# Agent attention and two MoE layers on one core: a query softmax with tokens on partitions, weight conversion in halves without GpSimd, filler products in the prologue

## The chip, the core and the metric

The kernel runs on one core of one Trainium2 chip. The metric is the device time of one execution in microseconds. Engines are named as in the profile: PE (TensorE) multiplies, PEld is its weight load, DVE (VectorE) and ACT (ScalarE) do elementwise work, POOL (GpSimd) does some of it too, and SP (SyncE) issues the DMAs.

## The reference

What is computed, cut to its core (12480 tokens, 128 channels, 49 agents, hidden width 2048):

```
def sm(a, b):                                  # softmax of scaled scores
    s = (a @ b.transpose(0, 2, 1)) / sqrt(128)
    s = s - s.max(-1, keepdims=True)
    e = exp(s)
    return e / (e.sum(-1, keepdims=True) + 1e-9)
agent_v = sm(agents, k) @ v                    # 49 x 128
x = sm(q, agents) @ agent_v                    # 12480 x 128
h = maximum(x @ w_in1, 0);  x = (h * h) @ w_out1
h = x @ w_in2;  g = maximum(h, 0) + alpha * minimum(h, 0);  out = g @ w_out2
```

The four weight matrices come as 64-bit floats; all else, and the output, is 32-bit.

## The kernel before, in words

The first stage computes the agent attention over k and v, 13 chunks of tokens (one of 192, twelve of 1024), with a running maximum. Its result, `avT`, is folded into the first weight matrix (`w1_product`: `agent_v @ w_in1`), so that the main loop starts from the softmax weights of the queries. The second layer's linear part (`alpha * h`) is folded into a small matrix M, the product of `w_in2` scaled by alpha with `w_out2` (`m_transpose`, `m_alpha`, `m_product`, `m_add`); `w_out2` itself is scaled by one minus alpha.

The main loop runs over 25 blocks of queries (320 tokens, 23 times 512, 384), each with 8 steps `s`. A step does four products on PE, in this order: `H1` (hidden of layer 1, 2 x 128 hidden units), `O1` (layer 1's output, two steps behind), `H2` (layer 2's hidden, eleven steps behind) and `O2` (layer 2's output, one behind `H2`). Every factor is split into a high and a low part in a 32-bit format for PE (`F32R`), and each product is the sum of three (low x high, high x low, high x high); a contraction uses 64 rows of the array, so two products run side by side (`mm2`, pairs of matmuls). Between them ACT does `R1` (relu), `SQ` (square) and `G2_hi`, and DVE does `G1_hi`, `G1_lo` and `G2_lo` (the splits).

The softmax weights of block b+1 are made during block b. The query tile has channels and agents folded onto 32-row groups: `q_transpose` (32x32 transposes on DVE), `q_split_hi`, `q_split_lo`, `q_scores` (six pairs of matmuls, 256 columns each), `q_squares` (two DVE transposes out of PSUM), `q_max` with `swap` (four small copies to exchange the halves of the agents), `q_sub`, `q_exp`, `q_sum` with `swap`, `q_norm`, `q_back` (transpose), `q_hi`, `q_lo`. The tables `before` and `after` at the end of the kernel say at which step of a block each stands.

Everything ahead of block 2 is written out by hand in the string `ORDER` (the prologue): one word for each step, run from left to right, and every engine gets its instructions in that order. There `K`, `V` load chunks, `T C S X P A E F M R` are the attention's steps on a chunk or group, `N0 N1 N2 vT vc W Y Z` its end and the folded weights, and a word such as `bwi2.1` is a step on a piece of a weight: `d` load, `a` and `b` the conversion of the 64-bit words to 32-bit floats (`w_abs` on ACT, three integer instructions of `w_bits` on DVE), `s` scale (POOL), `h` and `l` the high and low part (ACT; POOL, two of them on DVE), `v` swap of halves by DMA, `t y z w` the matrix M. A weight has four pieces of 512 columns. `H1_16` is the first step after `ORDER`.

PSUM has a two-bank tile for each of the tags `h1`, `h2`, `o1`, `o2`; the query scores use `h1`, so the next `H1` waits until they are read. POOL and DVE both work on the weights in SBUF during the prologue.

Of the kernel before, what the change touches and what calls it, by code (L numbers as in the profile page):

```python
# [19 lines left out]
def agent_attention_moe_kernel(  # L20
# [34 lines left out]
    GA = (NA + 1) // 2  # L55
# [71 lines left out]
    raw = Slots(stg, 6, [QW, 2], I32, "raw")  # L127
    mag = Slots(stg, 2, [QW], I32, "mag")
    wf = Slots(stg, 7, [QW], F32, "wf")

    def w_load(x):
        name, g = x.split(".")
        g = int(g)
        w, t_ = W_IN[name].bitcast(I32), raw.take(x)
        if name[:2] == "wi":
            nc.sync.dma_start(
                out=t_.rearrange("p n w -> p (n w)"), in_=w[:, g * QW * 2:(g + 1) * QW * 2],
            )
        else:
            nc.sync.dma_start(  # L140
                out=t_.rearrange("p (k c) w -> p k (c w)", c=C),
                in_=w.rearrange("(k p) c -> p k c", p=128)[:, 4 * g:4 * g + 4, :],
            )

    def w_abs(x):
        nc.scalar.activation(mag.take(x).bitcast(F32), raw.get(x)[:, :, 1].bitcast(F32), AF.Abs, scale=REBIAS)

    def w_bits(x, dst):
        lo, hi, a = raw.get(x)[:, :, 0], raw.get(x)[:, :, 1], mag.get(x)
        nc.vector.tensor_scalar(a, a, 3, None, op0=ALU.logical_shift_left)  # L150
        nc.vector.scalar_tensor_tensor(  # L151
            out=a, in0=hi, scalar=SIGN, in1=a, op0=ALU.bitwise_and, op1=ALU.bitwise_or
        )
        nc.vector.scalar_tensor_tensor(
            out=dst.bitcast(I32), in0=lo, scalar=29, in1=a, op0=ALU.logical_shift_right, op1=ALU.bitwise_or
        )
        raw.drop(x)
        mag.drop(x)

    with tc.manual_schedule(), ExitStack() as first:  # L160
# [3 lines left out]
        banks["early"] = early  # L164

# [60 lines left out]
        def q_load(b, queue=None):  # L226
            if b >= NB:
                return
            q_sb[b] = qp.tile([128, NT], F32, tag="q", name="q_sb", bufs=2)[:, :QB * NQS[b]]
            n = NQS[b] // 2  # L230
            for r in range(2):
                for i in range(2):
                    p = r * H + i * QB
                    for h in range(2):
                        (queue or nc.sync).dma_start(
                            out=q_sb[b][p:p + QB].rearrange("t (h j c) -> t h j c", h=2, c=QB)[:, h],
                            in_=qv[i][:, h, Q0[b] + r * n:Q0[b] + (r + 1) * n],
                        )

        def q_transpose(b):  # L240
            if b >= NB:
                return
            t_ = qp.tile([128, NT], F32, tag="qT", name="qT", bufs=2)[:, :QB * NQS[b]]
            nc.vector.transpose(t_, q_sb[b])
            q_sb[b] = t_

        def q_split_hi(b):
            if b >= NB:
                return
            qh_sb[b] = qp.tile([128, NT], F32R, tag="qh", name="qh", bufs=1)[:, :QB * NQS[b]]  # L250
            nc.scalar.copy(qh_sb[b], q_sb[b])

        def q_split_lo(b):
            if b >= NB:
                return
            ql_sb[b] = qp.tile([128, NT], F32R, tag="ql", name="ql", bufs=1)[:, :QB * NQS[b]]
            nc.vector.tensor_tensor(out=ql_sb[b], in0=q_sb.pop(b), in1=f32(qh_sb[b]), op=ALU.subtract)

        def q_scores(b):
            if b >= NB:  # L260
                return

            n = QB * NQS[b] // 2
            p_ = ps("h1", "s2_ps")[:, :, :n]
            qh, ql = qh_sb.pop(b), ql_sb.pop(b)
            mm2(
                lambda r: p_[:, r],
                [
                    lambda r, a=a, x=x, h=h: (a[rows(r), h], x[rows(r), h * n:(h + 1) * n])
                    for h in range(2) for a, x in ((agTl, qh), (agTh, ql), (agTh, qh))  # L270
                ],
            )
            s2_ps[b] = p_

        def swap(t_):

            for i in range(4):
                o = i ^ 1
                nc.vector.tensor_copy(t_[i * QB:(i + 1) * QB, 1, :], t_[o * QB:(o + 1) * QB, 0, :])

        def q_squares(b):
            if b >= NB:
                return

            s = qp.tile([128, NT // QB, QB], F32, tag="s2", name="s2", bufs=1)[:, :NQS[b]]
            p_ = s2_ps.pop(b)
# [100 lines left out]
        def w_hi(x):  # L387
            nc.scalar.copy(halves(x)[0], source(x))
# [588 lines left out]
```

## Time and profile before

| what | value |
|---|---|
| time, median of 3 runs | 1099.97 us (1099.87 to 1102.6) |
| profiled execution, its own time | 1100.91 us |
| span of the profiled execution | 1099.1 us |
| PE busy | 1069.3 us, 97% |
| DVE busy | 892.7 us, 81% |
| ACT busy | 732.4 us, 67% |
| POOL busy | 20.6 us, 2% |
| mean granted clock of PE | 0.99 |

How to read it: the span is the time from the first to the last instruction, and the execution's own time lies 1.81 us above it. Busy shares are averages over stages with different limits. The prologue takes about the first 126 us, the loop the rest. A matmul's duration in the trace includes its passage through the array, so that matmuls overlap; what one costs in a dense stretch is the distance from its start to the next one's start. A matmul of full 32-bit floats appears in the trace as two rows (a transpose as one), and a row with "x2" stands for two matmuls that run side by side.

### The profile page before, as it was taken

To read this page: it belongs to the slowest core of one execution; us is meant where nothing else is said; L and a number is where in the kernel's file an instruction comes from. 1 tells how busy PE (TensorE), PEld (TensorE's weight loads), DVE (VectorE), ACT (ScalarE), POOL (GpSimd) and SP (SyncE) were. 2 spreads that over 40 slices of the span, in tenths; PEclk is the share of its full clock that TensorE was granted. 3 is DMA by queue.
4 is the path that set the end of the run, shared out by engine and by line. 5 is a ranking of instruction groups with operands and counts; after the bars stand their busy time and mean duration, and the time that the engine had idled before them with its cause. 6 is when DMAs were issued, how large, how long until landed. Compare 5 with 4: busy or idle time off the path is not lost.

```text
span 1099.1 us, 22054 instructions
## 1 busy us (share of the span) xinstructions
PE 1069.3 (97%) x9352; PEld 855.5 (78%) x9352; DVE 892.7 (81%) x1375; ACT 732.4 (67%) x851; POOL 20.6 (2%) x20
## 2 busy tenths in 40 slices
PE   8968999999999999999999999999999999999997
PEld 5646878888888888888888888888888888888886
DVE  7988988788788888888888788788888878878743
ACT  5857766666666676666666766666666766766642
POOL 0033000000000000000000000000000000000000
PEclk9969999999999999999999999999999999999999
DMA  9942011111111111111111111111111111001111
GB/s 331 393 105 44 17 22 36 22 25 34 29 20 31 30 19 32 29 20 30 30 21 30 30 21 29 30 20 30 30 21 30 29 18 30 20 11 30 23 23 17
DMA packets 120314, 49.24 MB, mean 45 GB/s; under 512 B 103511, under 2 KB 110232, under 8 KB 120216
## 3 DMA queue, kind: packets, MB, share of 16 engines
q1 hardware_dynamic: 120216, 47.84, 18.0%
q8 instruction: 73, 1.20, 0.5%
q14 instruction: 25, 0.20, 0.1%
HBM read 27.59 MB, written 6.39 MB: 31 GB/s over the span
## 4 chain that ended last, share of the span: by engine, by line
PE 89%; DVE 5%; DMA 2%; issue 1%; ACT 1%; SPq 1%; DVEq 0%; ACTq 0%
PE o L78 50%; PE h_ps L78 36%; PE s_ps L78 2%; DVE g1l L771 2%; DMA raw<-in_moe_w_in_dram 1%; DVE g1h L766 1%; DMA ring<-in_k_dram 1%; PE av_ps L78 1%; PE kT_ps L525 1%; DVE g2l L847 0%; PE M_ps L78 0%; DMA q_sb<-in_q_dram 0%; DVE mag L151 0%; PE e_ps L568 0%; ACT kT L531 0%
## 5 line engine op out<-in xcount | busy, mean ns | idle before, releaser
L755 ACT ACTIVATE g<-h_ps 128x1024 f32<-128x1024 f32 (+2 forms) x200 | 201.1, 1006 | 164.6 <-PE h_ps L78 162.0
L841 ACT ACTIVATE g2h<-h_ps 128x1024 fp32r<-128x1024 f32 (+2 forms) x200 | 201.5, 1008 | 154.5 <-PE h_ps L78 134.3
L847 DVE SCALAR_TENSOR_TENSOR g2l<-h_ps,g2h 128x1024 fp32r<-128x1024 f32 (+2 forms) x200 | 238.2, 1191 | 23.0 <-ACT g2h L841 23.0
L771 DVE TENSOR_TENSOR g1l<-g,g1h 128x1024 fp32r<-128x1024 f32 (+2 forms) x200 | 243.0, 1215 | 6.8
L766 DVE CAST g1h<-g 128x1024 fp32r<-128x1024 f32 (+2 forms) x200 | 137.2, 686 | 104.6 <-ACT g L759 103.8
L759 ACT ACTIVATE g<-g 128x1024 f32<-128x1024 f32 (+2 forms) x200 | 207.8, 1039 | 6.2
L78 PE MATMUL o<-g1l,wo1h 64*128 64x512 f32 (+2 forms) x800 | 157.1, 389 | 4.9 <-DVE g1l L771 4.8
L78 PE MATMUL o<-g2l,wo2h 64*128 64x512 f32 (+2 forms) x800 | 157.8, 389 | 1.7 <-DVE g2l L847 1.7
L78 PE MATMUL o<-g1h,wo1l 64*128 64x512 f32 (+2 forms) x800 | 157.8, 391 | 0.5 <-DVE g1h L766 0.3
L78 PE MATMUL o<-g2h,wo2h 64*128 64x512 f32 (+2 forms) x800 | 158.1, 389 | 0.0
L78 PE MATMUL h_ps<-xh,wi2n 64*128 64x512 f32 (+2 forms) x800 | 157.4, 389 | 0.7 <-DVE g2l L847 0.7
L78 PE MATMUL h_ps<-sh,wi2s 64*128 64x512 f32 (+2 forms) x800 | 157.6, 388 | 0.4 <-DMA sh<-xh 0.4
L78 PE MATMUL o<-g2h,wo2l 64*128 64x512 f32 (+2 forms) x800 | 157.3, 388 | 0.0
L78 PE MATMUL o<-g1h,wo1h 64*128 64x512 f32 (+2 forms) x800 | 156.7, 388 | 0.0
L78 PEld LDWEIGHTS o<-g1l,wo1h 64*128 64x128 f32 x800 | 75.8, 186 | 23.7 <-DVE g1l L771 6.8
L78 PEld LDWEIGHTS o<-g2l,wo2h 64*128 64x128 f32 x800 | 76.2, 185 | 18.7 <-DVE g2l L847 2.1
L78 PEld LDWEIGHTS h_ps<-sh,wi2s 64*128 64x128 f32 x800 | 76.7, 185 | 17.9 <-DMA sh<-xh 0.9
L78 PEld LDWEIGHTS h_ps<-xh,wi2n 64*128 64x128 f32 x800 | 76.5, 185 | 18.1 <-DVE g2l L847 1.5
L78 PEld LDWEIGHTS o<-g2h,wo2l 64*128 64x128 f32 x800 | 76.6, 186 | 17.5 <-ACT g2h L841 0.4
L78 PEld LDWEIGHTS o<-g1h,wo1l 64*128 64x128 f32 x800 | 75.6, 186 | 18.5 <-DVE g1h L766 1.3
L78 PEld LDWEIGHTS o<-g2h,wo2h 64*128 64x128 f32 x800 | 76.3, 185 | 16.7
L78 PEld LDWEIGHTS o<-g1h,wo1h 64*128 64x128 f32 x800 | 75.8, 186 | 17.2
(139 smaller groups left out, 1290.4 us busy)
## 6 DMA issues: line engine op xcount, KB each, us to landing
ring<-in_k_dram SPq DMA_DIRECT2D x12, 512.0 KB, 9.2
ring<-in_v_dram SPq DMA_DIRECT2D x12, 512.0 KB, 10.2
sh<-xh SPq DMA_DIRECT2D x46, 128.0 KB, 2.4
sl<-xl SPq DMA_DIRECT2D x46, 128.0 KB, 2.3
out_dram<-ot SPq DMA_DIRECT2D x92, 64.0 KB, 2.0
q_sb<-in_q_dram SPq DMA_DIRECT2D x176, 32.0 KB, 1.9
raw<-in_moe_w_in_dram SPq DMA_DIRECT2D x8, 512.0 KB, 9.1
raw<-in_moe_w_out_dram SPq DMA_DIRECT2D x8, 512.0 KB, 10.3
```

The source lines that it names most:

```text
L78: nc.tensor.matmul(o, lhsT, rhs, start=start, stop=stop)
L525: nc.tensor.transpose(kT_ps[c][:, j // t, (j % t) * p:(j % t + 1) * p], t_[:p, j, :], ident[:p, :p])
L755: nc.scalar.activation(g, h1p.pop(s), AF.Relu)
L759: nc.scalar.activation(h1g[s], h1g[s], AF.Square)
L766: nc.vector.tensor_copy(gh, g)
L771: nc.vector.tensor_tensor(out=gl, in0=g, in1=f32(gh), op=ALU.subtract)
L841: nc.scalar.activation(gh, h2p[s], AF.Relu)
L847: nc.vector.scalar_tensor_tensor(out=gl, in0=p_, scalar=0.0, in1=f32(gh), op0=ALU.max, op1=ALU.subtract)
```

## The change

It has five parts.

1. The query softmax has tokens on partitions. `q_scores` is now, for each 128 tokens, one matmul of full 32-bit floats with the query tile as the stationary operand and 49 agents as columns. Maximum, subtraction, sum and division then run on 49 numbers along the free axis; the two splits of the query and all `swap` copies are gone. The weights are transposed back in 32x32 squares, split, and brought to the place that the loop expects by 16 DMAs for each block (`q_place`). Block 0 and 1 are transposed on PE instead.
2. Weights are converted in halves (1024 columns), not quarters. The sign, the magnitude and the scale come from one parametric ReLU on ACT (`w_rebias`, slope -2^32 for negative numbers), so that DVE needs two integer instructions for a half (`w_shift`, `w_low_bits`) and not three for a quarter.
3. No weight work is on POOL: scaling and the low parts are on DVE, as is the scaling by alpha; three of the high parts are on DVE, three on ACT.
4. Products of a zero tile (`keep_busy`, words `@n` in `ORDER`: n matmuls of 256 columns in a 16-bit format) are put into the prologue, 86 of them.
5. The 192-token chunk of k and v comes last, not first; four of the `G1_hi` of the prologue move to ACT (`HI_SCALAR`); and `ORDER` is written anew.

The diff, cut to what matters:

```diff
+    SMALL = 12
     def chunks(x):
...
+        whole.insert(SMALL, x[0][o:o + FIRST].rearrange("(p t) c -> p (t c)", t=TS))
...
+    NWARM = 18
+    UW, UC = DFF // 2, FC // 2
+    raw = Slots(stg, 3, [UW, 2], I32, "raw")
+    wf = Slots(stg, 4, [UW], F32, "wf")
+    mts = Slots(stg, 1, [UW], F32, "mT")
...
-    def w_abs(x):
-        nc.scalar.activation(mag.take(x).bitcast(F32), raw.get(x)[:, :, 1].bitcast(F32), AF.Abs, scale=REBIAS)
-    def w_bits(x, dst):
-        lo, hi, a = raw.get(x)[:, :, 0], raw.get(x)[:, :, 1], mag.get(x)
-        nc.vector.tensor_scalar(a, a, 3, None, op0=ALU.logical_shift_left)
-        nc.vector.scalar_tensor_tensor(
-            out=a, in0=hi, scalar=SIGN, in1=a, op0=ALU.bitwise_and, op1=ALU.bitwise_or
-        )
-        nc.vector.scalar_tensor_tensor(
-            out=dst.bitcast(I32), in0=lo, scalar=29, in1=a, op0=ALU.logical_shift_right, op1=ALU.bitwise_or
-        )
+        def w_rebias(x):
+            if x[:3] != "wi1":
+                wf.take(x)
+            nc.scalar.activation(
+                single(x), raw.get(x)[:, :, 1].bitcast(F32), AF.Prelu, scale=REBIAS, alpha=-(2.0 ** 32)
+            )
+        def w_shift(x):
+            a = single(x).bitcast(I32)
+            nc.vector.tensor_scalar(a, a, 3, None, op0=ALU.logical_shift_left)
+        def w_low_bits(x):
+            a = single(x).bitcast(I32)
+            nc.vector.scalar_tensor_tensor(
+                out=a, in0=raw.get(x)[:, :, 0], scalar=29, in1=a, op0=ALU.logical_shift_right, op1=ALU.bitwise_or
+            )
+            raw.drop(x)
...
         def q_scores(b):
             if b >= NB:
                 return
-            n = QB * NQS[b] // 2
-            p_ = ps("h1", "s2_ps")[:, :, :n]
-            qh, ql = qh_sb.pop(b), ql_sb.pop(b)
-            mm2(
-                lambda r: p_[:, r],
-                [
-                    lambda r, a=a, x=x, h=h: (a[rows(r), h], x[rows(r), h * n:(h + 1) * n])
-                    for h in range(2) for a, x in ((agTl, qh), (agTh, ql), (agTh, qh))
-                ],
-            )
-            s2_ps[b] = p_
+            n = count(b)
+            s2_ps[b] = ps("h1", "s2_ps")[:, 0, :n * H].rearrange("p (j a) -> p j a", a=H)[:, :, :NA]
+            t_ = q_sb.pop(b)
+            for j in range(n):
+                mm(s2_ps[b][:, j], t_[:, j * 128:(j + 1) * 128], agT[:, :NA])
+            e_sb[b] = e_pad[b % 2][:, :n]
...
+        def q_sum(b):
+            if b >= NB:
+                return
+            sm = small_q(b, "sm")
+            nc.vector.tensor_reduce(out=sm[:, :, 0], in_=q_weights(b), op=ALU.add, axis=AX.X)
+            nc.vector.tensor_scalar(sm, sm, 1e-9, None, op0=ALU.add)
+            nc.vector.reciprocal(sm, sm)
+            mx_sb[b] = sm
...
+        def q_place(b):
...
+            for u in range(4):
+                for g in range(2):
+                    for r in range(2):
+                        p = r * H + g * QB
+                        nc.sync.dma_start(
+                            out=f32(qs_sb[b][p:p + QB, :, u * n:(u + 1) * n]),
+                            in_=f32(t_[u * QB:(u + 1) * QB, :, g * n:(g + 1) * n]),
                         )
...
         def w_scale(x):
-            g = int(x[4:])
-            nc.gpsimd.tensor_tensor(
+            nc.vector.tensor_tensor(
...
+        HI_VECTOR = "wi2.0 wo1.0 wo1.1".split()
+        LO_POOL = "".split()
...
         def m_alpha(x):
+            g = unit(x)[1]
+            nc.vector.tensor_tensor(out=by_chunk(mts.take(g)), in0=wT.pop(x), in1=of_chunk(alp, g), op=ALU.mult)
...
+        def keep_busy(n):
+            if "loop" in banks:
+                p_ = banks["fill"][:, 1]
...
+            for _ in range(n):
+                mm(p_[:, :256], warm[:, :128], warm)
...
-            bwi2.3 vT vc hwi2.3 PART1 W0 awo2.1 bwo2.0 W1 Y0 Z0 swo2.0 awo2.3 bwo2.1 PART2 H1_0 Y1 q2 r1_0
+            fwi2.1 @15 vT vc hwi2.1 bwo2.0 PART1 @6 W0 fwo2.0 awo2.1 W1 Y0 bwo2.1 Y1 Z0 Z1 PART2 @10 H1_0 q2
...
         before = {
-            0: [(q_split_lo, 1)], 2: [(q_max, 1)], 3: [(q_sub, 1)], 4: [(q_sum, 1)], 5: [(q_norm, 1)],
-            6: [(q_back, 1)], 7: [(q_lo, 1), (q_transpose, 2)],
+            2: [(q_sum, 1)], 3: [(q_norm, 1), (q_back, 1)], 4: [(q_lo, 1), (q_place, 1)], 7: [(q_transpose, 2)],
         }
-        after = {3: [(q_exp, 1)], 6: [(q_hi, 1)], 7: [(q_split_hi, 2)]}
+        after = {1: [(q_exp, 1)], 3: [(q_hi, 1)]}
...
+        HI_SCALAR = [int(x) for x in "3 5 7 9".split()]
...
             if i == 1:
                 q_scores(b + 1)
-                q_squares(b + 1)
+                q_max(b + 1)
+                q_sub(b + 1)
```

What this does to the order of instructions is shown at three places. First PE, in the loop, at the second step of a block, where the scores of the next block stand between `O1` (tile `o`, weights `wo1h`) and `H2` (tile `h_ps`, weights `wi2n`). Before:

```order
L78 MATMUL o_2254<-g1h,wo1h 128x512 x2
L78 MATMUL s_ps<-qh,agTl 128x256 x2
L78 MATMUL s_ps<-ql,agTh 128x256 x2
L78 MATMUL s_ps<-qh,agTh 128x256 x2
L78 MATMUL s_ps<-qh,agTl 128x256 x2
L78 MATMUL s_ps<-ql,agTh 128x256 x2
L78 MATMUL s_ps<-qh,agTh 128x256 x2
L78 MATMUL h_ps<-xh,wi2n 128x512 x2
```

And now:

```order
L84 MATMUL o_1624<-g1l,wo1h 128x512 x2
L84 MATMUL o_1624<-g1h,wo1h 128x512 x2
L84 MATMUL s_ps<-agT,qT 128x49 x4
L84 MATMUL h_ps<-xh,wi2n 128x512 x2
L84 MATMUL h_ps<-xl,wi2n 128x512 x2
```

Twelve matmuls of 256 columns in six pairs have become four of 49 columns, each with stationary data of its own on all 128 rows.

Second DVE, in the prologue, from the last attention result (`avT`) to the first loop steps (`g1h`, `g1l`). `W1l` is the low part of the folded weight on which `H1_0` waits. Before:

```order
L633 COPY avT<-avT_ps 128x128
L150 TENSOR_SCALAR mag<-mag 128x512
L151 SCALAR_TENSOR_TENSOR mag<-raw,mag 128x512
L154 SCALAR_TENSOR_TENSOR wf<-raw,mag 128x512
L650 TENSOR_TENSOR W1l<-w_ps,W1h 128x512
L150 TENSOR_SCALAR mag<-mag 128x512
L151 SCALAR_TENSOR_TENSOR mag<-raw,mag 128x512
L154 SCALAR_TENSOR_TENSOR wf<-raw,mag 128x512
L650 TENSOR_TENSOR W1l<-w_ps,W1h 128x512
L395 TENSOR_TENSOR wo1l<-wf,wo1h 128x512
L766 CAST g1h<-g_849 128x2x320
L771 TENSOR_TENSOR g1l<-g_849,g1h 128x2x320
```

And now:

```order
L611 COPY avT<-avT_ps 128x128
L356 TENSOR_SCALAR wf<-wf 128x1024
L360 SCALAR_TENSOR_TENSOR wf<-raw,wf 128x1024
L356 TENSOR_SCALAR wf<-wf 128x1024
L627 TENSOR_TENSOR W1l<-fill_ps,W1h 128x512
L627 TENSOR_TENSOR W1l<-w_ps,W1h 128x512
L360 SCALAR_TENSOR_TENSOR wf<-raw,wf 128x1024
L413 TENSOR_TENSOR mT<-wT_ps,alp 128x1024
L782 CAST g1h<-g_792 128x2x320
L787 TENSOR_TENSOR g1l<-g_792,g1h 128x2x320
L782 CAST g1h<-g_813 128x2x320
L787 TENSOR_TENSOR g1l<-g_813,g1h 128x2x320
```

The pieces are twice as long, one of the three conversion instructions is gone, and the scaling of the transposed weight (`mT`) has come over from ACT.

Third SP's queue in the loop, one block: `q_sb` is the load of a query block, `sh` and `sl` the swapped halves of the second layer's input, `out_dram` the result, `qs` the placed softmax weights. Before:

```order
L235 DMA q_sb<-in_q_dram 32x8x32 x8
L807 DMA sh<-xh 64x512 x2
L807 DMA sl<-xl 64x512 x2
L865 DMA out_dram<-ot 32x16x32 x4
L235 DMA q_sb<-in_q_dram 32x8x32 x8
```

And now:

```order
L223 DMA q_sb<-in_q_dram 32x16x32 x4
L823 DMA sh<-xh 64x512 x2
L823 DMA sl<-xl 64x512 x2
L881 DMA out_dram<-ot 32x16x32 x4
L323 DMA qs<-hl 32x2x128 x16
```

A block has 28 issues on SP where it had 16; the sixteen new ones stand behind the output of the block before.

## Rows read from the trace of the kernel before

**Rows 1.** The page: busy time by engine; the chain that ended last, by engine.

```profile
PE 1069.3 (97%) x9352; PEld 855.5 (78%) x9352; DVE 892.7 (81%) x1375; ACT 732.4 (67%) x851; POOL 20.6 (2%) x20
...
PE 89%; DVE 5%; DMA 2%; issue 1%; ACT 1%; SPq 1%; DVEq 0%; ACTq 0%
```

**Rows 2.** Stretches: length, busy PE, PEld, DVE, ACT, POOL, granted clock, DMA share, GB/s.

```profile
180.00:1060.00 880.00, 880.00 (x7674) 710.75 (x7672) 726.17 (x1059) 597.18 (x647) 0.00 (x0) 1.00 0.14 26
...
68.36:126.14 57.78, 49.31 (x434) 39.07 (x435) 52.16 (x82) 41.52 (x66) 14.55 (x10) 0.91 0.17 34
...
40.00:50.00 10.00, 9.49 (x80) 6.07 (x81) 9.11 (x18) 8.86 (x16) 0.00 (x0) 1.00 1.04 393
...
70.00:75.00 5.00, 3.81 (x18) 2.40 (x18) 4.96 (x5) 3.43 (x8) 4.12 (x3) 0.50 0.00 0
```

**Rows 3.** Timeline of PE: the first H1 of the loop, and H1_16.

```profile
68.36 0.42 PE L78 MATMUL h_ps<-qsh,W1l 64*128 64x320 f32 x2 [1.46 <-DVE W1l L650]
...
126.14 0.39 PE L78 MATMUL h_ps<-qsh,W1l 64*128 64x512 f32 x2
```

**Rows 4.** Timeline of PE at a block's scores: start, duration, instruction.

```profile
538.48 0.40 PE L78 MATMUL o<-g1h,wo1h 64*128 64x512 f32 x2
538.72 0.28 PE L78 MATMUL s_ps<-qh,agTl 64*128 64x256 f32 x2
...
539.43 0.39 PE L78 MATMUL h_ps<-xh,wi2n 64*128 64x512 f32 x2
```

**Rows 5.** Timeline of PE and PEld at products and transposes of full 32-bit floats.

```profile
32.83 0.85 PEld L525 LDWEIGHTS kT_ps<-ident,ring 128*128 128x128 f32 x8 [0.17 <-issue]
...
7.47 0.78 PE L78 MATMUL qT_ps<-ident,q_nat 80*64 80x80 f32 x16
...
103.21 1.16 PE L78 MATMUL M_ps<-wf 128*128 128x128 f32 x8
104.29 0.50 PE L78 MATMUL h_ps<-qsh,W1l 64*128 64x512 f32 x2
104.63 0.40 PE L78 MATMUL h_ps<-qsl,W1h 64*128 64x512 f32 x2
```

**Rows 6.** Timeline of SP's queue in the loop: start and duration of the issues.

```profile
542.60 1.11 SPq L807 DMA_DIRECT2D sh<-xh  x2
```

**Rows 7.** Timeline at the attention's end: DVE and PE.

```profile
61.12 0.34 DVE L593 SCALAR_TENSOR_TENSOR acc<-acc,fac,av_ps 128x128 f32<-128x128 f32 x1
...
63.17 0.28 DVE L633 COPY avT<-avT_ps 128x128 f32<-128x128 f32 x1
...
63.50 3.40 PE L78 MATMUL w_ps<-wi,avT 128*64 128x512 f32 x8 [1.19 <-DVE avT L633]
```

**Rows 8.** Groups by shape on DVE: count, busy us, mean ns of one.

```profile
L771 DVE TENSOR_TENSOR g1l<-g,g1h 128x1024 fp32r<-128x1024 f32 x184 | 225.4, 1225 | 6.2
...
L766 DVE CAST g1h<-g 128x1024 fp32r<-128x1024 f32 x184 | 126.9, 690 | 96.8 <-ACT g L759 96.1
...
L847 DVE SCALAR_TENSOR_TENSOR g2l<-h_ps,g2h 128x640 fp32r<-128x640 f32 x8 | 6.5, 814 | 0.4 <-ACT g2h L841 0.4
...
L308 DVE TENSOR_TENSOR s<-s,m 128x250 f32<-128x250 f32 x1 | 0.4, 423 | 0.0
```

**Rows 9.** Timeline of DVE and POOL in the prologue.

```profile
73.08 1.51 POOL L395 TENSOR_TENSOR wi2n<-wf,wi2n 128x512 fp32r<-128x512 f32 x1
...
73.50 1.77 DVE L771 TENSOR_TENSOR g1l<-g,g1h 128x640 fp32r<-128x640 f32 x1
75.20 0.48 DVE L766 CAST g1h<-g 128x640 fp32r<-128x640 f32 x1
75.71 0.82 DVE L771 TENSOR_TENSOR g1l<-g,g1h 128x640 fp32r<-128x640 f32 x1
```

More of the change, by code (lines that the diff above doesn't have):

```diff
@@ L164, in agent_attention_moe_kernel @@
         banks["early"] = early
+        e_pad = [const.tile([128, 4, H], F32, name=f"e_pad{x_}") for x_ in range(2)]
+        for t_ in e_pad:
+            nc.vector.memset(t_, 0.0)
+        warm = const.tile([128, 256], BF16, name="warm")
+        nc.vector.memset(warm, 0.0)
         ident = const.tile([128, 128], F32, name="ident")
@@ L479, in kv_load @@
         def kv_load(x, c):
-            t_ = chunk(x, c) if c == 0 else ring.take((x, c))
+            t_ = chunk(x, c) if c == SMALL else ring.take((x, c))
             nc.sync.dma_start(out=t_.rearrange("p t c -> p (t c)"), in_=(kv if x == "k" else vv)[c])
         def kv_drop(x, c):
-            if c:
+            if c != SMALL:
                 ring.drop((x, c))
@@ L667, in q_turn, with q_first_copy @@
             q_ps[b] = ps("", "qT_ps")[:, 0, :4 * w]
-            for h in range(2):
-                for u in range(2):
-                    for r in range(2):
-                        o = (2 * h + u) * w
-                        mm(q_ps[b][rows(r), o:o + w], t_[:, 2 * r + u, rows(h)], ident[:w, :w])
+            for g in range(4):
+                nc.tensor.transpose(q_ps[b][:, g * w:(g + 1) * w], t_[:, g], ident[:w, :w])
+        def q_first_copy(b):
+            q_sb[b] = qp.tile([128, NT], F32, tag="qT", name="qT", bufs=1)[:, :QB * NQS[b]]
+            nc.scalar.copy(q_sb[b], q_ps.pop(b))
@@ new lines, in agent_attention_moe_kernel, with q_first_scores @@
+        e_first = [att.tile([128, 4, 2, H], F32, name=f"e_first{x_}") for x_ in range(2)]
+        for t_ in e_first:
+            nc.vector.memset(t_, 0.0)
+        def q_first_scores(b):
+            w = QB * NQS[b] // 4
+            s2_ps[b] = ps("", "s2_ps")[:w, 0, :4 * H].rearrange("p (j a) -> p j a", a=H)[:, :, :NA]
+            t_ = q_sb.pop(b)
+            for g in range(4):
+                mm(s2_ps[b][:, g], t_[:, g * w:(g + 1) * w], agT[:, :NA])
+            e_sb[b] = e_first[b][:w]
@@ new lines, in q_first_norm, with q_first_twice, q_first_back @@
+        def q_first_norm(b):
+            e, sm = e_sb[b], mx_sb.pop(b)
+            p = e.shape[0]
+            nc.vector.tensor_tensor(
+                out=e[:, :, 1, :NA], in0=e[:, :, 0, :NA], in1=sm.to_broadcast([p, 4, NA]), op=ALU.mult
+            )
+        def q_first_twice(b):
+            e = e_sb[b]
+            nc.scalar.copy(e[:, :, 0, :NA], e[:, :, 1, :NA])
+        def q_first_back(b):
+            w = QB * NQS[b] // 4
+            q_ps[b] = ps("", "qe_ps")[:, 0, :4 * w]
+            e = e_sb.pop(b)
+            for g in range(4):
+                nc.tensor.transpose(
+                    q_ps[b][:, g * w:(g + 1) * w], e[:, g].rearrange("p r a -> p (r a)"), ident[:w, :w]
+                )
```

396 lines of the change are left out of this document (169 added, 227 removed).

## Prediction

> **What bounds the kernel now.** I read the page first: PE is busy for 97% of the span and holds 89% of the chain that ended last [rows 1]. Then the stretches: from 180 to 1060 us PE has no idle microsecond at a granted clock of 1.00, with DVE at 726 of 880 us [rows 2]. There only PE's own work counts, and DVE's or ACT's savings are worth nothing. Between the first `H1` at 68.36 and `H1_16` at 126.14 [rows 3] it is otherwise: DVE is busy for 52.16 of 57.78 us (90%), PE shows 49.31 at a mean clock of 0.91 [rows 2], so the prologue is DVE's. The change has to be summed in two places: the prologue, which ends when `H1_16` starts, and the 972.96 us from there to the end of the span.
>
> **The loop: scores.** PE's cost of a step is the distance of starts: a pair of 512 columns takes 0.235 us, and the six pairs of the old scores 539.43 - 538.72 = 0.71 us [rows 4]. They go. In their place come four products of full 32-bit floats, each two rows, so eight weight loads of 128 columns with a stream of 49 columns behind each. No row has this shape. From below: streams alone, at the pace of the transposes with 80 columns (16 rows in 0.78 us, 0.049 each [rows 5]) give 8 x 0.049 = 0.39. From above: the M product's rows, 128 columns each, 104.29 - 103.21 = 1.08 us for eight. Between lies what I hold to be the limit, the load: eight of exactly this size took 0.85 us on PEld; two of the half-width loads of the 80-column transposes, at 2 x 0.049 each, would give 0.78 [rows 5]. A change of tile also costs something: behind the M product the first pair lasted 104.63 - 104.29 = 0.34 us and not 0.235, so 0.1 on the way out, and I put the same on the way in. So c = 0.80 + 0.20 = 1.00 us, with bounds 0.59 and 1.28. Scores of blocks 3 to 24 stand in this stretch, 22 of them: 22 x (1.00 - 0.71) = +6.4 us, between -2.6 and +12.5.
>
> The Trainium skill ("TensorE: Matmul & The Clock Gate", section "LDWEIGHTS (loading the stationary operand)") puts a load at the number of columns over 1.2, in ns, whatever the rows; 128 columns are 107 ns, and the eight loads in 0.85 us (106 ns each) agree [rows 5]. By that rule c would be 1.06, and the scores +7.6 us: it speaks against exchanging wide streams for many loads.
>
> **The loop: everything else.** The splits, copies and transposes that DVE and ACT lose are hidden behind PE today and bring nothing. `q_max` and `q_sub` now read `h1` in the place of two transposes; the next `H1` is twelve pairs away (2.8 us), which covers two instructions of at most 0.42 us each (the 250-element row [rows 8]). SP gets sixteen issues in a block behind `q_lo` of step 4. An issue takes half of 1.11 us [rows 6], so 8.9 us. From step 4 to the next block's first `H1` are four steps of 21 pairs, 19.7 us; what waits behind them on SP is the next query load, which is needed a block later. I count this at nothing; uncovered, each microsecond late would cost 22.
>
> **The prologue: its start.** All of `w_in2` is now loaded ahead of the last full v chunk, whose last quarter came behind it before: one load of 128 x 1024 words (0.52 MB) more, at 393 GB/s [rows 2] 1.3 us later. Against that the last chunk to be multiplied has 192 tokens, not 1024, and no POOL work slows DVE there. The last update of `acc` was at 61.12 [rows 7]; nothing in the trace shows how far the smaller chunk brings it forward, so I bound it by 62.4 (only the later load) and 58.5 (the load outweighed three times) and take 60.0. From there to `H1_0` it was 7.24 us. Of these the folded product took 3.40 at a granted clock of about 0.5 and falls to 1.7 if the fillers hold the clock; the conversion between `acc` and `avT` (61.46 to 63.17, three instructions) becomes one of 1.2, 0.6 less. So 4.9 us, and `H1_0` at 65.0, the second `W1l` done at 65.5.
>
> **The prologue: DVE.** From `W1l` to the `G2_lo` of `H2_4`, DVE's new queue holds 58 instructions. By shape: nine of 1024 elements on weights (one `w_low_bits`, four low parts, two scalings by 1 - alpha, two by alpha) and eight `G1_lo`, 17 x 1.225 = 20.8; seven `G1_hi` x 0.69 = 4.8 [rows 8]; eight `G1_lo` of 640, 0.82 each = 6.6, and five `G1_hi`, 0.48 each = 2.4 [rows 9]; five `G2_lo` x 0.814 = 4.1; two transposes at 0.69 = 1.4; eight pieces of the softmax and six small ones for x and M at 0.42 = 5.9 [rows 8]. Sum 46.0 us. The durations are those without POOL: while POOL works, a `G1_lo` takes 1.77 and not 0.82 us [rows 9], and with no weight work on POOL that stretch is gone. `H1_16` does not wait for the last `G2_hi` and `G2_lo` (1.5 us). So 65.5 + 46.0 - 1.5 = 110.0 if DVE never waits, and 115.1 if it is busy for 90%, as before.
>
> **The prologue: PE.** From `H1_0` to `H1_16`: 126 pairs of 320 columns at 0.147 (0.235 x 320/512) = 18.5, 60 pairs of 512 = 14.1, sixteen transposes of the weights (0.135 a row and 0.4 for the changes) 2.6, two M products of sixteen rows 4.7, scores 1.0; 45 fillers of 256 columns (0.118) with six changes of tile 6.5. Sum 47.4, and `H1_16` at 112.4 if every filler counts and nothing waits. PE and DVE are now nearly level. I take 112.0, between DVE's ends and beside PE's sum: 14.1 us before the old 126.14.
>
> **The sum.** 112.0 + 972.96 + 6.4 = 1091.4 us of span, plus the 1.81 us outside it, 1093.2 against the profiled execution's 1100.91. The median of the runs stands 0.94 us below that: 1092.2.
>
> **Rivals.**
> *More from the prologue, cheap scores.* DVE's queue without waits and c at 0.63: 108.8 + 972.96 - 1.8 + 0.87 = 1080.8. For it: the fillers need not count, where PE would idle anyway. Against: DVE waited for 10% before.
> *The fillers don't hold the clock.* From 70 to 75 us the clock was 0.50 with PE busy for 3.81 us [rows 2], 1.9 lost; with the folded product's 1.7 again at half speed this takes back 3.6: 1095.8. For it: DVE's instructions still come in long runs between PE's.
> *The scores pay load and stream one after the other* (slower). Place: PE in the loop, once a block. Each row then costs 0.106 for its load and 0.098 for its stream (two of the 80-column rows, which ran side by side): 8 x 0.204 + 0.2 = 1.83, and 22 x 1.12 = +24.7 us: 1110.5. The prologue's 14.1 us are used up at c = 1.35, and from c = 1.50 the kernel is slower. Against it: the M product has the same loads and a longer stream, and its rows follow each other in 0.135 us.
> The Trainium skill (same page, section "The mechanism") says that loads overlap running matmuls only where their row groups differ; all of these use all rows, so by that rule this rival is the case. The 0.135 us is less than a load of 0.106 and a stream of 128 columns (0.059 at the least, half of a 256-column pair) one after the other, so the trace is against it.
> *Placed weights come late.* From issues of 1.2 us on (16 x 1.2 = 19.7 us) `H1` waits once a block; at 1.5 us it waits 4.3 us, 95 us in all. The 0.55 us are against it.
> *The change doesn't do what it says*: that scores stay cheap and the prologue stays at 126 (DVE waits where it was busy): 1106 with c = 1.00.
>
> **How the numbers follow.** Changes under 0.3% (3.3 us) can't be told from none here. Chances: forecast 0.58 (own range 1085 to 1098, from `H1_16` at 108 to 115 and c from 0.85 to 1.1), more from the prologue 0.17, clock 0.11, serial scores 0.07, late weights 0.03, prologue unmoved 0.04. Faster (under 1096.7): 0.50 + 0.17 + 0.06 = 0.73. Within 0.3%: 0.07 + 0.05 + 0.02 = 0.14. Slower (over 1103.3): 0.01 + 0.05 + 0.03 + 0.04 = 0.13. The range 1080 to 1103 leaves out the slow rivals and a little at the fast end.
>
> **What would show it.** In the new profile: `H1_0` near 65 and the folded product in 1.7 us at clock 1.00; no DVE instruction of 640 elements over 0.9 us; `H1_16` near 112; the scores' distance in the loop 1.0 us with no idle PE from there on; the sixteen placements of a block issued in about 9 us. The prediction is wrong if PE waits in the loop, if c lies above 1.35, or if `H1_16` comes later than 119.

## The result, and the profile after

The changed kernel takes 1071.96 us (median of 4 runs, 1071.42 to 1072.8) against 1100.83 (1099.87 to 1102.6) for the kernel before on the same chip: a ratio of 0.9737, 95% interval 0.972 to 0.9753, 28.9 us less. The forecast was 1092.2, with a range from 1080 to 1103. The direction was right; the time lies 8.0 us under the range. One execution of 1507.9 us among those of `a_pool` below, at a mean granted clock of 0.65 (the others: 0.99 and more), is left out of its median.

The page of the changed kernel, busy time by engine and the chain by engine:

```profile
PE 1053.3 (98%) x9324; PEld 863.8 (81%) x9324; DVE 775.5 (72%) x1008; ACT 706.2 (66%) x798; POOL 0.7 (0%) x6
...
PE 95%; DMA 3%; DVE 1%; ACT 1%; issue 0%; SPq 0%; DVEq 0%; ACTq 0%
```

VectorE has lost 117 us of work, GpSimd nearly all of its own, and PE still sets the end [rows 1]. Three stretches of the changed kernel: the prologue from `H1_0` to `H1_16`, everything from there to the end, and the loop:

```profile
65.05:112.70 47.65, 47.43 (x474) 40.35 (x475) 40.97 (x57) 36.48 (x47) 0.00 (x0) 1.00 0.23 50
112.70:1070.19 957.49, 947.40 (x8356) 783.24 (x8352) 693.42 (x859) 627.02 (x681) 0.00 (x0) 1.00 0.18 38
...
130.00:1000.00 870.00, 870.00 (x7614) 715.66 (x7612) 645.40 (x800) 585.88 (x631) 0.00 (x0) 1.00 0.19 39
```

In the prologue PE is now busy for 47.43 of 47.65 us at a granted clock of 1.00, where it was at 0.91 before, and VectorE for 40.97: PE bounds it [rows 2]. `H1_16` starts at 112.70 and not 126.14 [rows 3]: 13.4 us. But from `H1_16` on the changed kernel takes 957.49 us where the kernel before took 1099.1 - 126.14 = 972.96: 15.5 us less, although each block's scores became dearer. In the loop PE is without a gap in both. So PE itself has become faster. The rows that answer to [rows 4], PE around one block's scores, changed kernel:

```profile
557.09 0.39 PE L84 MATMUL o<-g1l,wo1h 64*128 64x512 f32 x2
557.32 0.39 PE L84 MATMUL o<-g1h,wo1h 64*128 64x512 f32 x2
557.63 1.09 PE L84 MATMUL s_ps<-agT,qT 128*128 128x49 f32 x8
558.66 0.50 PE L84 MATMUL h_ps<-xh,wi2n 64*128 64x512 f32 x2
558.99 0.39 PE L84 MATMUL h_ps<-xl,wi2n 64*128 64x512 f32 x2
...
571.03 0.39 PE L84 MATMUL h_ps<-qs,W1l 64*128 64x512 f32 x2
...
573.08 0.39 PE L84 MATMUL h_ps<-xh,wi2n 64*128 64x512 f32 x2
```

From 571.03 to 573.08 are nine pairs: 0.228 us each. The same nine pairs of the kernel before, in one of its blocks, take 0.234 each:

```profile
552.08 0.40 PE L78 MATMUL h_ps<-qsh,W1l 64*128 64x512 f32 x2
...
554.19 0.39 PE L78 MATMUL h_ps<-xh,wi2n 64*128 64x512 f32 x2
```

Over all pairs of 512 columns in the loop (distances over 260 ns, at the scores or behind a wait, left out) the mean distance of starts is 227.0 ns now and 234.2 before, the same within 0.1 ns in every stretch of 40 us from 180 to 980. A block has 171 such pairs and 22 blocks lie in the loop: 22 x 171 x 7.2 ns = 27 us. That is the gain that the forecast lacks. The question for the experiments is what makes the same products, at the same granted clock, 3% faster.

The trace of before held a sign of it. Pairs of 320 and of 384 columns there, in the first blocks and in the last:

```profile
129.12 0.31 PE L78 MATMUL o<-g2h,wo2l 64*128 64x320 f32 x2
129.27 0.31 PE L78 MATMUL o<-g2l,wo2h 64*128 64x320 f32 x2
129.41 0.31 PE L78 MATMUL o<-g2h,wo2h 64*128 64x320 f32 x2
...
1044.61 0.34 PE L78 MATMUL o<-g1h,wo1l 64*128 64x384 f32 x2
1044.79 0.34 PE L78 MATMUL o<-g1l,wo1h 64*128 64x384 f32 x2
1044.96 0.34 PE L78 MATMUL o<-g1h,wo1h 64*128 64x384 f32 x2
```

They follow each other in 0.147 and 0.173 us (means over groups of six: 146.7 and 173.3 ns). The line through both gives 226.7 ns for 512 columns; the trace showed 234.

### The profile page after: what moved, and what is told of

Its sections match the earlier page's. It is cut to its first block, busy times and chain, and to the rows that moved or that the text cites. A ratio compares the mean times of both kernels' runs of the same rounds, so it can differ in the third digit from the quotient of the medians.

```text
span 1070.2 us, 22037 instructions
## 1 busy us (share of the span) xinstructions
PE 1053.3 (98%) x9324; PEld 863.8 (81%) x9324; DVE 775.5 (72%) x1008; ACT 706.2 (66%) x798; POOL 0.7 (0%) x6
## 4 chain that ended last, share of the span: by engine, by line
PE 95%; DMA 3%; DVE 1%; ACT 1%; issue 0%; SPq 0%; DVEq 0%; ACTq 0%
PE o L84 51%; PE h_ps L84 38%; PE s_ps L84 3%; DMA ring<-in_k_dram 1%; PE fill_ps L84 1%; DMA raw<-in_moe_w_out_dram 1%; DMA raw<-in_moe_w_in_dram 1%; PE kT_ps L503 1%; PE av_ps L84 1%; DMA sl<-xl 0%; ACT g2h L857 0%; PE e_ps L546 0%; PE wT_ps L409 0%; ACT kT L509 0%; DVE wf L356 0%
## 5 line engine op out<-in xcount | busy, mean ns | idle before, releaser
L782 DVE CAST g1h<-g 128x1024 fp32r<-128x1024 f32 (+2 forms) x196 | 133.8, 682 | 182.4 <-ACT g L770 179.5
L787 DVE TENSOR_TENSOR g1l<-g,g1h 128x1024 fp32r<-128x1024 f32 (+2 forms) x200 | 239.7, 1199 | 6.9 <-ACT g1h L780 0.3
L84 PE MATMUL o<-g2l,wo2h 64*128 64x512 f32 (+2 forms) x800 | 155.1, 383 | 0.5 <-DVE g2l L863 0.5
L84 PE MATMUL h_ps<-sh,wi2s 64*128 64x512 f32 (+2 forms) x800 | 155.1, 382 | 0.4 <-DMA sh<-xh 0.3
L84 PE MATMUL o<-g2h,wo2l 64*128 64x512 f32 (+2 forms) x800 | 155.0, 382 | 0.0
L84 PE MATMUL o<-g2h,wo2h 64*128 64x512 f32 (+2 forms) x800 | 154.8, 382 | 0.0
L84 PE MATMUL o<-g1h,wo1l 64*128 64x512 f32 (+2 forms) x800 | 154.4, 382 | 0.0
L84 PE MATMUL o<-g1l,wo1h 64*128 64x512 f32 (+2 forms) x800 | 153.8, 381 | 0.0
L84 PE MATMUL o<-g1h,wo1h 64*128 64x512 f32 (+2 forms) x800 | 153.8, 381 | 0.0
L84 PE MATMUL h_ps<-qs,W1h 64*128 64x512 f32 (+2 forms) x800 | 121.3, 381 | 0.0
## 6 DMA issues: line engine op xcount, KB each, us to landing
ring<-in_v_dram SPq DMA_DIRECT2D x12, 512.0 KB, 10.5
```

The source lines that it names most:

```text
L84: nc.tensor.matmul(o, lhsT, rhs, start=start, stop=stop)
L782: nc.vector.tensor_copy(gh, g)
L787: nc.vector.tensor_tensor(out=gl, in0=g, in1=f32(gh), op=ALU.subtract)
```

## Experiments

Each time is a median, beside the kernel before on the same chip. In most of these kernels no instruction is changed: a tile only gets more columns, which nothing uses, so that the tiles allocated behind it move. In the built programs all weights of the loop start 128 bytes beyond a multiple of 256 bytes of their partition, in both kernels. The tiles that are streamed against them (`qs`, `g1h`, `xh`, ...) are allocated behind `notpad`, a column of 4 bytes that takes 32: in the kernel before they start 32 bytes beyond a multiple of 256, in the changed kernel 128 beyond. Two edits of the change make that difference. `notpad` is left away, which alone would bring them to a multiple of 256, 128 off the weights. And the small tiles of the softmax, for the maximum and the sum (`m`, `sm`), have shrunk from 768 bytes to 128, which moves them by 128 more (mod 256).

**The first round: is it the address, VectorE's load, or the new scores?**

`b_align`, the kernel before:
```
- notpad = const.tile([128, 1], F32, name="notpad")
+ notpad = const.tile([128, 16], F32, name="notpad")[:, :1]
```


> The kernel before; the column notpad is stored in 64 bytes and not 4, so that every tile behind it starts on a multiple of 64 bytes of its partition (before: 32 beyond one). No instruction is changed. Address theory (a pair of 512 columns takes 234.2 ns where its streamed operand starts 32 bytes beyond a multiple of 64, 227.0 where it starts on one): pairs at 227, 22 blocks x 171 pairs x 7.2 ns = 27 us less, 1074. DVE-load theory (PE's pairs are slowed by what DVE and ACT do beside them): pairs stay at 234, 1101. Theory of the new scores (their full-row products put PE into a faster rhythm): 1101.


Measured: 1096.45 (ratio 0.9967, 0.9956 to 0.9979), pairs at 233.3 ns. The address theory in this form, with a granule of 64 bytes, fell.

`a_shift32`, the changed kernel:
```
- alp = const.tile([128, FC], F32, name="alp")
+ alp = const.tile([128, FC + 8], F32, name="alp")[:, :FC]
```


> The changed kernel; the tile alp is 32 bytes longer, so that all tiles behind it start 32 bytes beyond a multiple of 64. No instruction is changed. Address theory: pairs of 512 columns go from 227.0 to 234.2 ns, 1099. The other two theories: 1072.


Measured: 1096.32 (0.9964, 0.9949 to 0.9979), pairs at 233.3 ns: 32 bytes of padding cost 24 us. The other two theories fell here.

`a_x32`, the changed kernel: the tile `x` is `[128, NT + 8]`.


> The changed kernel; the tile x, first of its pool, is 32 bytes longer, so that xh, sh, xl and sl (streamed by H2 and by the product with M) start 32 bytes beyond a multiple of 64, and all other streamed tiles stay on one. Address theory, of the streamed operand: H2 at 234, H1, O1 and O2 at 227; 22 x 51 pairs x 7.2 ns = 8.1 us, 1080. If the address of something else in the kernel mattered: all pairs alike. The other two theories: 1072.


Measured: 1082.54 (0.9842, 0.9826 to 0.9859). PE in one step of it:

```profile
577.31 0.39 PE L84 MATMUL o<-g1h,wo1l 64*128 64x512 f32 x2
...
578.67 0.40 PE L84 MATMUL h_ps<-xh,wi2n 64*128 64x512 f32 x2
...
580.07 0.39 PE L84 MATMUL o<-xh,Ml 64*128 64x512 f32 x2
```

Six pairs of `O1` take 1.36 us (226.7 ns each), six of `H2`, the only moved ones, 1.40 (233). So it is the place of the streamed tile that slows its pairs. The six `O2` pairs behind `H2`, whose streams did not move, are slowed a little too (230.5 ns in the mean), and the expectation lacked them (1080).

`a_dve`, the changed kernel:
```
+ for _ in range(2 if s >= 2 * NP and s % NP in (1, 4, 6) else 1):
      nc.vector.tensor_tensor(out=gl, in0=g, in1=f32(gh), op=ALU.subtract)
```


> The changed kernel, with three of the eight G1_lo of each block from block 2 on done twice (the same values written again): 3 x 1.2 us more of DVE in a block, which brings DVE's busy share in the loop back to that of before (0.74 to 0.83). Address theory: 1072. DVE-load theory: pairs back to 234, 1099.


Measured: 1116.8 (1.0146, 1.0131 to 1.0161), a miss for both theories in time. The pairs themselves keep 226.7 ns, so VectorE's load doesn't set their pace. What is lost is a wait, by the list of waits from 300 to 1000 us (total us, times, longest):

```profile
PEld h_ps L84 <- DVE g2l L864: 38.6, 50, 1.1
PE h_ps L84 <- DVE g2l L864: 19.5, 33, 0.7
```

Three such waits in a block (50 of the weight loads in 16.7 blocks; 33 of them leave PE idle too) make a block 41.94 us long and not 39.97. `H2` waits for `G2_lo` of the step before, which frees its accumulator; a second `G1_lo` of 1.2 us, three in a block, makes that late. There the slack of VectorE is less than one instruction long, though in the changed kernel it idles for 26% of the loop.

**The second round: the granule.**

`b_align128`: `notpad` is `[128, 32]`, 128 bytes.


> The kernel before; notpad is stored in 128 bytes, so that all streamed tiles start on a multiple of 128 bytes, as they do in the changed kernel (with 64 bytes in its place they started 64 beyond one, and pairs took 233.3 ns). No instruction is changed. Granule theory (a pair of 512 columns takes 227 ns if its streamed operand starts on a multiple of 128 bytes, else 233 to 234): 22 blocks x 171 pairs x 7.2 ns = 27 us less, 1073. Rival, that the rhythm needs the new scores or the lighter VectorE as well: pairs stay at 233, 1096.


Measured: 1078.76 (0.9808, 0.9793 to 0.9822), pairs at 227 to 228. That is 20.9 us less than the kernel before on the same chip, by 96 bytes of padding. From `H1_16` to the end it takes

```profile
126.39:1077.04 950.65, 941.32 (x8446) 776.27 (x8442) 785.36 (x1146) 645.91 (x702) 0.00 (x0) 1.00 0.13 26
```

950.65 us, 22.3 less than before, with VectorE as busy as ever. The pairs alone would be worth 27. A part of the rest is a wait, once in a block, which neither the kernel before nor the changed one has (list from 180 to 1000 us, and one block):

```profile
PEld h_ps L78 <- DVE g2l L847: 6.5, 20, 0.3
...
577.84 1.22 DVE L847 SCALAR_TENSOR_TENSOR g2l<-h_ps,g2h 128x1024 fp32r<-128x1024 f32 x1
...
578.83 0.39 PE L78 MATMUL o<-g1h,wo1h 64*128 64x512 f32 x2
...
579.11 0.50 PE L78 MATMUL h_ps<-xh,wi2n 64*128 64x512 f32 x2
579.45 0.40 PE L78 MATMUL h_ps<-xl,wi2n 64*128 64x512 f32 x2
```

`H2` starts 0.05 us after the end, at 579.06, of the `G2_lo` that frees its accumulator: 0.28 us after the pair ahead of it and not 0.227. Its first pair then takes 0.34. With a few slower pairs behind, that costs 0.20 us a block (mean of 20), 21 times: 4.2 us. So with pairs at 227 ns the work that VectorE has in the kernel before is no longer quite hidden.

`a_shift64`: `alp` is `[128, FC + 16]`.


> The changed kernel; alp is 64 bytes longer, so that all streamed tiles start 64 bytes beyond a multiple of 128, and Mh and Ml, which held that offset, now start on one. Granule theory with 128 bytes: pairs at 233.3 ns, 1096. If 64 bytes were enough in this kernel: 1072.


Measured: 1085.53 (0.9873, 0.9859 to 0.9888), pairs between 229 and 232: slower, by less than expected.

`a_all128`: `alp` and `oma` are `[128, FC + 16]` each.


> The changed kernel; alp and oma are 64 bytes longer each: streamed tiles start on multiples of 256 bytes (before: 128 beyond one), and the weights Mh and Ml on multiples of 128 (before: 64 beyond one). Granule theory for streamed operands alone: all as in the changed kernel, 1072, the pairs with M too (235 ns). If stationary operands have the same granule: the three pairs with M fall to 227, 22 x 3 x 8 ns = 0.5 us. If a coarser granule counts: all pairs below 226.7 ns.


Measured: 1091.4 (0.9923, 0.9906 to 0.9939). All three expectations missed: streamed tiles on multiples of 256 bytes are slow (232.3 ns). But look at the product with M:

```profile
584.43 0.39 PE L84 MATMUL o<-xh,Ml 64*128 64x512 f32 x2
584.65 0.39 PE L84 MATMUL o<-xl,Mh 64*128 64x512 f32 x2
584.88 0.40 PE L84 MATMUL o<-xh,Mh 64*128 64x512 f32 x2
585.11 0.40 PE L84 MATMUL o<-g2h,wo2l 64*128 64x512 f32 x2
585.36 0.40 PE L84 MATMUL o<-g2l,wo2h 64*128 64x512 f32 x2
```

Its first two pairs take 227 ns (medians over the loop: 227, 227, 232). Beside each of these two streams PE loads `Mh`, which here starts on a multiple of 256 as `xh` and `xl` do; beside the third it loads `wo2l`, 128 bytes off. In the changed kernel it is the other way: all is fast except these pairs and the three behind them, and there `Mh` and `Ml` are the weights that lie off (192 beyond a multiple of 256, the streams 128):

```profile
574.21 0.39 PE L84 MATMUL h_ps<-sh,wi2s 64*128 64x512 f32 x2
574.43 0.40 PE L84 MATMUL o<-xh,Ml 64*128 64x512 f32 x2
574.67 0.39 PE L84 MATMUL o<-xl,Mh 64*128 64x512 f32 x2
574.90 0.40 PE L84 MATMUL o<-xh,Mh 64*128 64x512 f32 x2
575.14 0.39 PE L84 MATMUL o<-g2h,wo2l 64*128 64x512 f32 x2
```

The medians over the loop are 236, 231 and 236. That made a new theory: what counts is the distance, modulo 256 bytes, between the operand that streams and the weights that are loaded meanwhile. The word "meanwhile" is not shown: the pair ahead of these three, beside which `Ml` is loaded, keeps 226 ns, and the third, beside which `wo2l` is loaded, takes 236, though `wo2l` lies where the streams do.

**The third round: the distance.**

`a_rel64`, the changed kernel; `warm`, ahead of all weights, is 64 bytes longer:


> The changed kernel; the tile warm, which stands ahead of all weights, is 64 bytes longer, so that weights and streamed tiles alike lie 64 bytes further on; their distance stays a multiple of 256. No instruction is changed. Theory of the distance (a pair of 512 columns takes 226.7 ns if the streamed operand and the weights that are loaded meanwhile lie a multiple of 256 bytes apart, else 229 to 236): all as in the changed kernel, 1072. Theory of the streamed operand's own address (it must start 128 bytes beyond a multiple of 256; here it is 192): pairs at 230 to 233, 1085 to 1096.


Measured: 1072.34 (0.9741, 0.9726 to 0.9756), pairs at 227.0. Streamed tiles at 192 are as fast as at 128 if the weights move along. The theory of the operand's own address fell.

`b_w160`, the kernel before; `ident`, ahead of the weights, is 160 bytes longer, `notpad` 96:


> The kernel before; ident, which stands ahead of all weights, is 160 bytes longer, and notpad 96 bytes longer, so that the weights start 32 bytes beyond a multiple of 256 and not 128, and the streamed tiles stay where they were, 32 beyond one. No instruction is changed. Theory of the distance: the streamed tiles now lie a multiple of 256 bytes from the weights, pairs at 227 ns as with notpad of 128 bytes, 1079. Theory of the streamed operand's own address: pairs stay at 234 ns, 1100.


Measured: 1076.86 (0.9786, 0.9772 to 0.9801). Its pairs, with streamed tiles 32 beyond a multiple of 256 as ever:

```profile
573.32 0.39 PE L78 MATMUL h_ps<-qsh,W1l 64*128 64x512 f32 x2
...
574.00 0.39 PE L78 MATMUL o<-g1h,wo1l 64*128 64x512 f32 x2
```

Three pairs in 0.68 us, 227 ns each: the kernel before becomes fast if only its weights change their place relative to the streams. Together:

| streams minus weights, mod 256 bytes | kernels | mean pair of 512, ns |
|---|---|---|
| 0 | after, a_rel64, b_align128, b_w160 | 227.0 to 227.2 |
| 32 | a_shift32 | 233.3 |
| 64 | a_shift64 | 229 to 232 |
| 128 | a_all128 | 232.3 |
| 160 | before | 234.2 |
| 192 | b_align | 233.3 |

`a_qM`, the changed kernel padded so that `Mh`, `Ml` and `qT` fit as well:


> The changed kernel with padding (alp and oma 192 bytes longer each, the small tiles of the softmax 64 bytes in the place of 32), so that Mh and Ml, and qT, the stationary operand of the scores, also lie a multiple of 256 bytes from what is streamed beside their loads (they lay 64 and 128 off it). Theory of the distance: the three pairs with M at 227 ns and not 231 to 236, 22 x 0.02 us = 0.5 us; the pairs around the scores lose their 5 to 10 ns, up to 0.1 us a block; the scores by at most 0.2 us a block: 1067 to 1071. Theory of the streamed operand alone: 1072.


Measured: 1073.37 (0.9744, 0.9724 to 0.9764). The three pairs with M are at 227 now, as expected, but that is too little to be seen in the time; the scores and the pairs around them did not change by more than a nanosecond. The rule holds for the pairs, not for the scores' single products.

**The prologue.**

`a_nofill`, the changed kernel without the `@` entries of the order:


> The changed kernel without the products that keep TensorE busy (the @ entries of the order; those at the very start stay). Theory of the prediction, that they hold the clock: the clock falls between 56 and 80 us, the folded product takes 3.4 us and not 2, H1_16 comes at 113 to 117, 1072 to 1077. Rival, that the clock would hold without them and they only cost PE's time: H1_16 up to 6.5 us earlier, 1066.


Measured: 1068.8 (0.9724, 0.9709 to 0.9738). Each theory is right about the clock in one place:

```profile
60.00:65.00 5.00, 4.51 (x15) 1.41 (x16) 3.71 (x7) 3.25 (x4) 0.00 (x0) 0.56 0.49 80
65.00:70.00 5.00, 4.20 (x40) 3.42 (x42) 4.93 (x7) 3.85 (x6) 0.00 (x0) 1.00 0.04 6
...
80.00:85.00 5.00, 4.29 (x46) 3.62 (x46) 4.96 (x8) 4.77 (x6) 0.00 (x0) 1.00 0.25 51
```

At the folded product the clock falls to 0.56 and the product takes 3.7 us (60.35 to 64.03) and not 1.9. From `H1_0` on the clock stays at 1.00 without the fillers, with PE busy for 84% to 94% up to 85 us, and `H1_16` comes 45.67 us after `H1_0`, not 47.65.

`a_pre`: the `@` entries up to the folded product stay, the later ones go.


> The changed kernel, of whose busy-keeping products only those up to the folded product stay; tiles lie as in the changed kernel. Theory, that these alone are needed and the later ones cost 2 us: H1_16 is 45.6 us after H1_0 and not 47.65, 1068 to 1070. Rival, that the gain of the kernel with both edits came from its padding: 1072.


Measured: 1067.8 (0.9705, 0.9689 to 0.9721); `H1_16` 45.58 us after `H1_0`. That the fillers up to the folded product pay in the whole time is not shown: they hold its clock (1.94 us and not 3.7), but `H1_0` comes at 63.97 here and at 64.17 in `a_nofill`, and the intervals of the two kernels overlap. `a_best` is the same with the padding of `a_qM`:


> As a_qM, and of the products that keep TensorE busy only those up to the folded product stay; those from just before H1_0 on are left away. Theory, that these hold the clock of the folded product alone and later only cost PE's time: folded product 2 us, H1_0 at 63.9, H1_16 at 109, no stretch from there below a clock of 1.00; 3 us under a_qM. Rival, that the later ones hold the clock too: a clock below 1.00 between 65 and 90 us and no gain.


Measured: 1067.55 (0.9703, 0.9686 to 0.972), no rival's clock loss: 1.00 in every stretch from 50 to 110 us. Both beat the two kernels given, the changed one by some 4 us; the padding adds nothing that can be told.

`a_pool`, the changed kernel:
```
- LO_POOL = "".split()
+ LO_POOL = "wo1.0 wo1.1 wi2.0 wi2.1 wo2.0 wo2.1".split()
```


> The changed kernel with the low parts of the six halves of wo1, wi2 and wo2 on POOL and not on VectorE. Prediction's step (POOL slows VectorE: a subtraction of 640 elements took 1.77 and not 0.82 us beside it): VectorE is relieved of 6 x 1.2 = 7 us and pays up to 10 us, H1_16 at 113 to 118, 1073 to 1078. Rival, that POOL's work runs beside VectorE's at no cost: no VectorE instruction of 640 elements over 0.9 us, H1_16 at 112 or earlier.


Measured: 1075.55 (0.9777, 0.9749 to 0.9805; median of three executions, 1073 to 1079). VectorE beside POOL:

```profile
83.24 1.54 DVE L787 TENSOR_TENSOR g1l<-g,g1h 128x640 fp32r<-128x640 f32 x1 [1.45 <-ACT g1h L780]
...
85.21 0.83 DVE L787 TENSOR_TENSOR g1l<-g,g1h 128x640 fp32r<-128x640 f32 x1
```

One subtraction takes 1.54 and the next 0.83, as in [rows 9]. But only three pieces of POOL's work fall behind `H1_0`, and `H1_16` comes 48.15 us after it, half a microsecond more than with none (at 115.72, within the expected 113 to 118). More is lost ahead of `H1_0`:

```profile
61.04 3.12 POOL L392 TENSOR_TENSOR wi2n<-wf,wi2n 128x1024 fp32r<-128x1024 f32 x1 [10.14 <-ACT wi2n L387]
...
62.65 2.05 DVE L356 TENSOR_SCALAR wf<-wf 128x1024 int32<-128x1024 int32 x1 [0.71 <-ACT wf L350]
...
65.36 2.29 PE L84 MATMUL fill_ps<-warm 128*128 128x256 bf16 x10 [2.54 <-DVE W1l L627]
```

Beside POOL's subtraction VectorE's shift, which stands ahead of `W1l` in its queue, takes 2.05 us and not 0.69. PE stands still for 2.54 us, and the ten fillers behind take 2.29 us, at a clock of 0.50, and not 1.25. `H1_0` comes at 67.58, 4.8 us after the end of the folded product, and not 2.3. So POOL's work slows VectorE where PE waits for it, and the clock adds to that. How much of the 3 us in the median this is stays open, since `H1_0` lies anywhere from 64.6 to 68.1 in the traces of the changed kernel and of seven with the same prologue.

## Why the prediction was wrong, step by step

**The loop: everything else.** This is the step that failed. The prediction said that the work VectorE and ScalarE lose "brings nothing" and carried the 972.96 us from `H1_16` on over as they were. It took PE's pace for a property of the products. By leaving `notpad` away and making the small tiles of the softmax smaller, the change moved every streamed tile to a multiple of 256 bytes from the weights of its products (only `Mh` and `Ml` are off), and that took the pairs from 234.2 to 227.0 ns, 27 us by their number, 22.3 us as measured in the kernel before. That VectorE's work doesn't set the pairs' pace is right (`a_dve`: 226.7 ns with more of it). But "brings nothing" holds only at the old pace: with fast pairs and all the old work PE waits for VectorE once a block, 4.2 us in all (`b_align128`). The diff shows the removed tile, but no row of a duration says where tiles lie. What could have been read was that 320, 384 and 512 columns don't lie on one line.

**The scores** were sized too low. By the rows c is 557.32 to 558.99, 1.67 us, less two pairs of 0.227: 1.2 us and not 1.00, within its bounds (1.03 for the eight rows, 0.08 on the way in, 0.1 on the way out). The six old pairs cost 0.74 in `b_align128` (568.74 to 569.48 in one block), so at equal distances the exchange costs 0.48 us a block with the pairs around it, +10.5 us and not the +6.4 forecast. From `H1_16` on the changed kernel takes only 6.8 us more than `b_align128` (957.49 against 950.65), since the wait of 4.2 us falls away; that this is near 6.4 is chance. The miss of the loop is then -27 us for the pairs and +4 for the scores, against 21.9 measured (979.4 forecast, 957.49), with 1 us not accounted for. Load and stream of a row are not paid one after the other: that would have been 1.83.

**The prologue's start.** `H1_0` came at 65.05, forecast 65.0, by terms that were off against each other:

```profile
58.31 0.34 DVE L571 SCALAR_TENSOR_TENSOR acc<-acc,fac,av_ps 128x128 f32<-128x128 f32 x1
...
59.70 0.28 DVE L611 COPY avT<-avT_ps 128x128 f32<-128x128 f32 x1
...
60.79 1.08 PE L84 MATMUL fill_ps<-wi,avT 128*64 128x512 f32 x4
61.70 1.03 PE L84 MATMUL w_ps<-wi,avT 128*64 128x512 f32 x4
63.87 1.25 PE L84 MATMUL fill_ps<-warm 128*128 128x256 bf16 x10 [1.14 <-DVE W1l L627]
```

The last update of `acc` is at 58.31, not 60.0 (in seven other traces with the same prologue it lies between 58.4 and 61.9, so this may be the spread). The folded product takes 1.94 us at full clock, 1.7 forecast [rows 7]. And ten fillers stand between `W1l` and `H1_0`, 1.2 us that the working put nowhere. That `H1_0` agrees within 0.1 us is luck, the more so as it lies between 64.6 and 68.1 in those traces.

**The prologue's rest.** PE's own sum was 47.4 us from `H1_0`, measured 47.65 (47.65 to 47.83 in the eight traces); `H1_16` 112.70, forecast 112.0 (112.5 to 115.8). VectorE's was 46.0, measured 40.97. The long instructions' durations were right (39.9 in sum), and the fourteen small ones take 4.7 and not 5.9; but the sum added durations, and each instruction starts a little before the one ahead of it ends (2.2 us in all; visible in [rows 9], 75.20 against 73.50 + 1.77). The last `G2_lo`, 0.8, falls behind the stretch. That PE and VectorE were "nearly level" is therefore wrong. The fillers were priced at 6.5 us of PE's queue; without them `H1_16` comes only 2 us earlier, since PE then waits in their place (`a_pre`), and behind `H1_0` they hold nothing. The subtractions of 640 elements take 0.82 us with POOL idle, as forecast.

**SP.** The sixteen placements take more than the 8.9 us counted, and are still hidden:

```profile
576.38 10.29 SPq L323 DMA_DIRECT2D qs<-hl  x16
588.04 1.92 SPq L223 DMA_DIRECT2D q_sb<-in_q_dram  x4
```

0.64 us each here, 0.72 in the next two blocks, and PE has no gap in the loop. The rivals of late weights and of serial scores did not happen. Two slips in the working change none of this: 16 x 1.2 is 19.2 and not 19.7, and the first rival starts from 108.8 where DVE's queue without waits gave 110.0, so it would be 1082.0.

## What to carry to other kernels

Where TensorE is the bound, compare its pace over widths before taking it as given: if one width lies off the line of the others, look at where the streamed tiles and the weights lie in their partitions. Put them a multiple of 256 bytes apart, by padding a small tile, and keep odd columns of 4 bytes behind the tiles that are streamed. This is shown for pairs of 64 rows with 512 columns; the scores, single products over all rows, did not change with it (`a_qM`). In the changed kernel the distance was right by accident, from two edits that were made for other reasons. A change that adds or drops any tile moves all those behind it, so compare two kernels at equal distances before crediting the change: the kernel before, padded, takes 1078.76 us, and only some 7 us remain for the whole change (to 1071.96). And when the bounding engine becomes faster, look again for waits on engines that were hidden.

## What was not expected of the hardware

A pair of 512-column products on two halves of the rows takes 226.7 ns when the streams and the weights lie a multiple of 256 bytes apart; at the five other distances tried the kernels' means are 229 to 234.2; pairs of 320 and 384 columns took 146.7 and 173.3 ns in the kernel before, at a distance that slows 512. The Trainium skill ("SBUF — State Buffer", section "SBUF: two separate sides") says that TensorE's port never waits on anyone, and that among the engines only the port pair shared by VectorE and GpSimd is contended. The runs agree as far as other engines go (226.7 ns under more VectorE work; 1.54 and not 0.83 us on VectorE beside POOL). A conflict of TensorE's two own reads, which that section doesn't speak of, would fit the rest, but it is argued, not shown: the runs show the distance alone. Why 64 bytes cost less than 32 or 192 stays open.
